# Last pass of a two-layer decode step with gradients: transposes of X one item later, V transposes, dq and gradients ahead of the products

## The chip, the cores and the metric

The kernel runs on one core of a Trainium2 chip. The metric is the device time of one execution in microseconds (us). The core has five engines that matter here: TensorE (PE in the profile; its weight loads are shown as PEld), VectorE (DVE), ScalarE (ACT), GpSimd (POOL) and SyncE (SP). Each works through its own list of instructions in the order in which it was built. Transfers between device memory and the core's on-chip memory (SBUF) are issued by SP, ACT and POOL and carried out by 16 DMA engines. TensorE writes to PSUM only; VectorE and ScalarE copy from there to SBUF (an "evacuation").

## What is computed

The reference runs two kinds of layer in turn, twice each (attention, feed-forward, attention, feed-forward), on one token, and then takes the gradient of the whole with respect to the inputs, the two caches and the weights.

```
x = x + A(layernorm(x))      # A: 32 query heads, 4 groups of 8 heads, caches K and V of 4 x 65536 x 128, weights wq, wo
x = x + B(layernorm(x))      # B: squared ReLU between w1 and w2
x = x + A(layernorm(x))
x = x + B(layernorm(x))
returns x and, for the incoming gradient grad_out, the gradients of x, K, V, wq, wo, w1, b1, w2, b2
```

Both attention layers use the same K and V, so the gradient of a cache is a sum of both layers' parts. K and V hold 67 MB each in bf16, and their gradients as much again: moving these is most of what the kernel does.

## The kernel before, in words

The kernel goes over the caches in passes: forward through layer 1 and layer 3, then backward through layer 3 (`attn_bwd3`), then a last pass, `attn_bwd4` (line 1050), which finishes layer 1 and writes the gradients of K and V for both layers. The change is in that last pass, which begins near 1198 us of the profiled execution and lasts to its end.

The last pass handles 4 groups of heads, and in each group 512 chunks of 128 cache rows, 8 chunks to an **item**: 64 items to a group and 256 in all. Four items make a **block** of 32 chunks (`UB4`, line 67), 64 blocks in all. A block's data comes as one load of 1 MB of V and one of 1 MB of K, issued on SP's queue (line 284) into areas that are used in turn (five, for most of the pass). What happens to an item:

- `vT` (line 1095): 8 transposes of V on TensorE into a PSUM tile `ps_tr` (line 1100), then one evacuation to one of three buffers (`small<-ps_tr`, lines 155 and 158).
- `vS` (line 1105): 8 matmuls of the transposed V with the output gradients of both layers, the **products**, into the one PSUM tile `ps_sc` (line 1123); a block's first product is preceded by one matmul that sets the tile to minus a correction (line 1114). After a block's last product, X, a 128 x 1024 tile in one of two buffers, is made of it: VectorE multiplies the products with the stored exponentials (lines 1132 and 1133) into one half, and GpSimd copies the exponentials themselves (lines 1134 and 1135) into the other half.
- `xT` (line 1141): once to a block, 8 transposes of X into a `ps_tr` tile (line 1146) and an evacuation. `ps_tr` has two buffers, shared with `vT`.
- `dq` (line 1151): 8 matmuls of K with X, summed over the group in PSUM (line 1163).
- `grads` (line 1178): 4 matmuls of transposed X with a small matrix (line 1191), two each into the two `ps_gg` tiles, each evacuated to a staging area (as f32 to bf16: `pair<-ps_gg` and `eT<-ps_gg`). After a block's last item the staged gradients of K and V leave as two stores of 1 MB on POOL's queue (lines 1211 and 1212).

The order of the program is that of `pipeline` (line 659): at each step i it calls each stage with item i less the stage's lag, in the order in which the stages are listed. Before, the list (line 1228) is `vT` with lag 0, `vS` with lag 2, and `k8` (which is `dq` and then `grads`) with lag 7; `xT` is called at the end of `vS` for a block's last item. The first items are called by hand (`opening`, line 1222), with the flag `opening` keeping `xT` out of `vS`. Between the steps come background tasks: rows of weights are fetched on ACT's or POOL's queue and multiplied on VectorE (line 433) and summed on ScalarE (line 434), and the weight gradients are made by small matmuls (lines 1244 and 1271) into the same two `ps_gg` tiles and stored from staging areas on POOL's queue (line 1275). Such a task is tied in behind what stands before it on its engine (`in_order`, line 640).

The program's order is not yet that of the engines. A planner takes it as a priority and, with estimated durations, writes each engine's list, so an instruction whose data it reckons late is passed by others. Which of VectorE and ScalarE makes an evacuation is decided in `evac` (line 145) as the program is written out, by two running sums of estimated load.

Of the kernel before, what the change touches and what calls it, by code (L numbers as in the profile page):

```python
# [18 lines left out]
def kernel(  # L19
# [47 lines left out]
    UB4 = 512 // R2  # L67
    IPG = C // 8
    TLEAD = 2
# [19 lines left out]
    def ps_tr():  # L89
        return PS["pool"].tile([P, 8, P], BF, name="ps_tr", tag="tr", bufs=2 if PS["pass4"] else 3)  # L90

    def ps_sc(shape):
        return PS["pool"].tile(shape, F32, name="ps_sc", tag="sc", bufs=1 if PS["pass4"] else 2)
# [51 lines left out]
    def evac(out, in_, kind="bf"):  # L145
        n = 1
        for d in in_.shape[1:]:
            n *= d
        if kind == "bf":
            ca, cd = 0.19 + n * 0.00081, 0.15 + n * 0.00053  # L150
        else:
            ca, cd = 0.19 + n * 0.00081, 0.15 + n * 0.00105
        if load["act"] + ca <= load["dve"] + cd:
            load["act"] += ca
            nc.scalar.copy(out=out, in_=in_)  # L155
        else:
            load["dve"] += cd
            nc.vector.tensor_copy(out=out, in_=in_)  # L158

    def add_load(act=0.0, dve=0.0):  # L160
        load["act"] += act
        load["dve"] += dve
# [477 lines left out]
    def in_order(fn, each=False):  # L640

        insts = nc.cur_bb.bb.instructions
        n0 = len(insts)
        before = {}
        fn()
        new = list(insts[n0:])
        want = {i.engine for i in new}
        k = n0 - 1
        while want - set(before) and k >= max(0, n0 - 4000):
            before.setdefault(insts[k].engine, insts[k])  # L650
            k -= 1
        for i in new:
            p = before.pop(i.engine, None)
            if p is not None:
                tc.add_manual_dep(i, p.name, NOSYNC, reason="in_order")
            if each:
                before[i.engine] = i

    def pipeline(n, stages, bg=None, done=()):
        maxlag = max(l for _, l in stages)  # L660
        for i in range(n + maxlag):
            for k, (fn, lag) in enumerate(stages):
                if (done[k] if done else 0) <= i - lag < n:
                    fn(i - lag)
            for fn in (bg or {}).pop(i, ()):
                in_order(fn)
        assert not bg, sorted(bg)

    def items_of(order, turn=0):

        return [(g, (c8 + (turn if g == order[0] else 0)) % C) for g in order for c8 in range(0, C, 8)]
# [378 lines left out]
    def attn_bwd4(La, Lb, oga, ogb, order, eTa, eTb, dqT, bg, group_done, streams, more_stage, tail, KT, vts):  # L1050
        lname = "B1"
        kit = items_of(order)
        n = len(kit)
# [7 lines left out]
        state = {("vt", idx): vt for idx, vt in enumerate(vts)}  # L1061
        kstream, vstream = streams

        def g_scores(g):
            sl = slice(g * R, (g + 1) * R)
            ndt4 = state[("ndt", g)] = NDT.next()
            nc.vector.tensor_copy(out=DOB[:, g, 0, 0:R], in_=oga.dOT[:, sl])
            nc.vector.tensor_copy(out=DOB[:, g, 0, R:R2], in_=ogb.dOT[:, sl])
            nc.vector.tensor_copy(out=ndt4[:, :, 0:R], in_=oga.nd2[:, sl].unsqueeze(1).to_broadcast([64, UB4, R]))
            nc.vector.tensor_copy(out=ndt4[:, :, R:R2], in_=ogb.nd2[:, sl].unsqueeze(1).to_broadcast([64, UB4, R]))  # L1070
# [34 lines left out]
        def vS(idx):  # L1105
            g, c8 = kit[idx]
            vt = state.pop(("vt", idx))
            for i in range(8):
                c = c8 + i
                slot = c % UB4  # L1110
                first = idx < UB4 // 8

                def minus(**flags):
                    nc.tensor.matmul(state["ps_dp"][:, :, :].rearrange("p c r -> p (c r)"), lhsT=sel2[:, :],
                                     rhs=state[("ndt", g)][:, :, :].rearrange("o c r -> o (c r)"), **flags)
                if slot == 0:
                    state["ps_dp"] = ps_sc([P, UB4, R2])
                    if not first:
                        minus(start=True, stop=False)
                ps_dp = state["ps_dp"]  # L1120
                last = slot == UB4 - 1
                w = min(4, UB4 - slot)
                nc.tensor.matmul(ps_dp[:, slot:slot + w, :].rearrange("p a b -> p (a b)"), lhsT=vt[:, i, :],  # L1123
                                 rhs=DOB[:, g, 0:w, :].rearrange("p a b -> p (a b)"), start=first and slot == 0, stop=last and not first, skip_group_check=first)
                if last:
                    if first:
                        minus(start=False, stop=True, skip_group_check=True)
                    c0 = c - slot
                    X = XS.next().rearrange("p (s r) -> p s r", r=R4)
                    ea = eTa[g][:, :, c0:c0 + UB4].rearrange("p h c -> p c h")  # L1130
                    eb = eTb[g][:, :, c0:c0 + UB4].rearrange("p h c -> p c h")
                    nc.vector.tensor_tensor(out=X[:, :, 0:R], in0=ps_dp[:, :, 0:R], in1=ea, op=ALU.mult)
                    nc.vector.tensor_tensor(out=X[:, :, R:R2], in0=ps_dp[:, :, R:R2], in1=eb, op=ALU.mult)
                    nc.gpsimd.tensor_copy(out=X[:, :, R2:3 * R], in_=ea)
                    nc.gpsimd.tensor_copy(out=X[:, :, 3 * R:R4], in_=eb)
                    add_load(dve=2 * (0.07 + UB4 * R * 0.0021))
                    state[("X", g, c0 // UB4)] = X
                    if not state.get("opening"):
                        xT(g, c0 // UB4)

        def xT(g, u):
            X = state[("X", g, u)]
            nblk = UB4 // 4
            pt2 = ps_tr()
            for bi in range(nblk):
                nc.tensor.transpose(pt2[:, bi, :], X[:, 4 * bi:4 * bi + 4, :].rearrange("p a b -> p (a b)"), ident_b[:, :])  # L1146
            xt = XT.next()
            evac(xt[:, 0:nblk, :], pt2[:, 0:nblk, :])
            state[(g, u)] = (X, xt)
# [67 lines left out]
        for i, a in zip((36, 2 * IPG + 14, n - 18), [pair[10]] + more_stage):  # L1217
            at(bg, i, lambda a=a: ST.areas.append(a))
        g0 = order[0]
        state["opening"] = True  # L1220
        g_scores(g0)
        opening = [(g_grads, g0), (vS, 0), (vT, 3), (vS, 1), (vT, 4), (vS, 2), (vT, 5), (vS, 3), (vT, 6), (xT, g0, 0), (grads, 0), (vS, 4),
                   (grads, 1), (vT, 7), (vS, 5), (grads, 2), (dq, 0), (dq, 1), (grads, 3), (dq, 2), (dq, 3)]
        assert len(vts) == 3 and UB4 == 4 * 8
        for fn, *args in opening:
            in_order(lambda: fn(*args), True)
        state["opening"] = False
        pipeline(n, [(vT, 0), (vS, TLEAD), (k8, TLEAD + UB4 // 8 + 1)], bg, (8, 6, 4))


    def rows_into(rows, cols, nj, twice=False):
# [190 lines left out]
    bg = {}  # L1422
# [170 lines left out]
    bg = {}  # L1593
# [31 lines left out]
    def the_end():  # L1625
        PS["end"] = True
        with tc.high_priority():
# [5 lines left out]
    last_tasks = gwq_tasks(ORD4[-1:], False)  # L1633
    after = [2, 0, 0, 1, 1, 1, 1, 1]
    attn_bwd4(L1, L3, og1, og3, ORD4, eT1, eT3, dqT1, bg, group_done, streams, more_stage,
              lambda i: [t for _, t in zip(range(after[i]), last_tasks)], KT4, vts)
    PS["last"] = True
# [34 lines left out]
```

## Time and profile before

| | us |
|---|---|
| median of 3 runs | 1976.6 (1975.8 to 1980.17) |
| the profiled execution's own time | 1977.79 |
| its span in the trace | 1976.0 |
| TensorE busy in the span | 1588.3 (80%) |
| VectorE busy | 1106.1 (56%) |
| ScalarE busy | 1032.0 (52%) |
| GpSimd busy | 206.2 (10%) |
| moved by DMA | 802.40 MB, mean 406 GB/s |

The span is what the trace covers; 1.8 us of the execution's own time lie around it. Busy times overlap, since the engines work side by side. A view by stage gives, for a stretch of the span, each engine's busy time with its number of instructions, the TensorE clock that was granted (1.00 is full speed), the mean busy share of the 16 DMA engines and the rate at which they moved data. A view of waits lists which engine's instructions of a line stood idle until which other instruction ended. A timeline lists the instructions of a stretch, runs of one kind merged, with the idle time before each and what ended it.

### The profile page before, as it was taken

What the parts mean: (1) busy time and instruction counts of PE and PEld (TensorE: products, weight loads), DVE (VectorE), ACT (ScalarE), POOL (GpSimd) and SP (SyncE); (2) the same over time, 40 slices, a digit from 0 to 9 for tenths busy, and PEclk for the clock granted to TensorE, in tenths of its full rate; (3) what the DMA queues carried; (4) which work ended last, traced back from release to release, by engine and by line L of the source; (5) the groups of instructions that cost most, each with busy time, mean ns of one, the idle gap of its engine ahead of it and who ended that gap; (6) DMA issues with size and microseconds to landing.
All of it is one profiled execution on the core that took longest, in us unless ns stands there. A gap on an engine that the chain in (4) does not pass through costs nothing. (4 is left out here: it accounts for less than half of the span.)

```text
span 1976.0 us, 65950 instructions
## 1 busy us (share of the span) xinstructions
PE 1588.3 (80%) x29997; PEld 1307.1 (66%) x30052; DVE 1106.1 (56%) x1823; ACT 1032.0 (52%) x1306; POOL 206.2 (10%) x370
## 2 busy tenths in 40 slices
PE   7887886579887857887878887888888878888886
PEld 6887775578787756777878775555555545445553
DVE  4544431146444313736454445787776678777876
ACT  3543332034433323435454446776776666677775
POOL 0000000000000000000000001223222222122222
PEclk9999998669999986999989987999999989898987
DMA  9999999989999999999999997999999999999998
GB/s 394 425 423 420 414 410 408 408 334 425 425 420 419 424 406 400 423 418 416 417 417 392 412 404 319 373 417 424 423 422 416 414 373 402 421 380 398 422 424 360
DMA packets 115651, 802.40 MB, mean 406 GB/s; under 512 B 11420, under 2 KB 11434, under 8 KB 57002
## 3 DMA queue, kind: packets, MB, share of 16 engines
q1 hardware_dynamic: 77530, 612.54, 75.2%
q0 software_dynamic: 29776, 170.94, 21.1%
q10 hardware_dynamic: 8064, 14.68, 2.0%
q8 instruction: 235, 3.85, 0.8%
q14 instruction: 46, 0.38, 0.0%
HBM read 628.18 MB, written 169.95 MB: 404 GB/s over the span
## 5 line engine op out<-in xcount | busy, mean ns | idle before, releaser
L158 DVE COPY small<-ps_tr 128x1024 bf16<-128x1024 bf16 x620 | 420.9, 688 | 306.0 <-PE ps_tr L747 178.4
L155 ACT COPY small<-ps_tr 128x1024 bf16<-128x1024 bf16 x385 | 386.7, 1014 | 373.2 <-PE ps_tr L747 210.1
L155 ACT CAST pair<-ps_gg 128x1024 bf16<-128x1024 f32 (+3 forms) x279 | 267.7, 972 | 124.7 <-PE ps_gg L1191 78.4
L158 DVE CAST pair<-ps_gg 128x1024 bf16<-128x1024 f32 (+2 forms) x213 | 252.7, 1189 | 108.0 <-PE ps_gg L1191 84.2
L747 PE MATMUL ps_tr<-ident_b,pair 128*128 128x128 bf16 x3328 | 245.7, 222 | 40.7 <-DMA pair<-in_A_k_cache_dram 32.1
L1191 PE MATMUL ps_gg<-pair,small 64*128 64x512 bf16 x1024 | 203.5, 407 | 54.6 <-ACT pair L155 14.5
L747 PEld LDWEIGHTS <-pair 128*128 128x128 bf16 x3328 | 196.0, 99 | 46.6 <-DMA pair<-in_A_k_cache_dram 36.0
L809 PE MATMUL ps_acc<-eT,pair 128*128 128x64 bf16 x3840 | 169.0, 204 | 45.8 <-DMA pair<-in_A_v_cache_dram 42.7
L1100 PE MATMUL ps_tr<-ident_b,pair 128*128 128x128 bf16 x2024 | 185.4, 229 | 16.4 <-DMA pair<-in_A_v_cache_dram 11.0
L766 PE MATMUL ps_sc<-L_qpad,small 128*128 128x64 bf16 (+7 forms) x3456 | 171.2, 192 | 19.9 <-ACT small L155 11.5
L809 PEld LDWEIGHTS <-pair 128*128 128x128 bf16 x3840 | 152.4, 103 | 50.0 <-DMA pair<-in_A_v_cache_dram 45.8
L1100 PEld LDWEIGHTS <-pair 128*128 128x128 bf16 x2024 | 130.5, 102 | 75.7 <-issue 57.7
L766 PEld LDWEIGHTS <-small 128*128 128x128 bf16 x3456 | 137.7, 98 | 31.9 <-ACT small L155 17.9
L434 ACT ACTIVATE pair<-pair 128x1024 bf16<-128x1024 bf16 (+1 forms) x105 | 118.5, 1130 | 43.7 <-DVE pair L433 42.7
L1191 PEld LDWEIGHTS <-small 64*128 64x128 bf16 x1024 | 58.7, 94 | 113.0 <-issue 84.4
L999 PE MATMUL ps_tr<-ident_b,pair 128*128 128x128 bf16 x1536 | 122.7, 229 | 12.8 <-DMA pair<-in_A_v_cache_dram 5.9
L999 PEld LDWEIGHTS <-pair 128*128 128x128 bf16 x1536 | 97.3, 103 | 30.5 <-issue 21.0
L1020 PE MATMUL ps_sc<-B_dOpad,small 128*128 128x64 bf16 (+7 forms) x2048 | 104.1, 194 | 15.6 <-DVE small L158 6.5
L1123 PE MATMUL ps_sc<-DOB,small 128*128 128x64 bf16 (+3 forms) x2048 | 113.1, 196 | 1.8 <-ACT small L1543 1.2
L155 ACT CAST eT<-ps_gg 128x1024 bf16<-128x1024 f32 (+1 forms) x92 | 90.9, 991 | 41.1 <-PE ps_gg L1191 13.8
L1123 PEld LDWEIGHTS <-small 128*128 128x128 bf16 x2048 | 89.1, 101 | 32.8 <-issue 27.4
L1163 PE MATMUL ps_acc<-small,pair 128*128 128x64 bf16 (+1 forms) x2048 | 107.3, 195 | 0.4
(293 smaller groups left out, 2060.3 us busy)
## 6 DMA issues: line engine op xcount, KB each, us to landing
pair<-in_A_v_cache_dram SPq DMA_DIRECT2D x74, 2048.0 KB, 20.0
pair<-in_A_k_cache_dram SPq DMA_DIRECT2D x63, 2048.0 KB, 20.4
out_dram<-pair POOLq DMA_DIRECT2D x104, 1024.0 KB, 18.0
pair<-in_A_v_cache_dram SPq DMA_DIRECT2D x80, 1024.0 KB, 11.6
pair<-in_A_k_cache_dram SPq DMA_DIRECT2D x78, 1024.0 KB, 10.5
eT<-in_A_k_cache_dram SPq DMA_DIRECT2D x21, 2048.0 KB, 20.7
eT<-in_A_v_cache_dram SPq DMA_DIRECT2D x12, 2048.0 KB, 27.1
out_dram<-eT POOLq DMA_DIRECT2D x41, 512.0 KB, 17.1
```

Source lines behind the costliest of these rows:

```text
L155: nc.scalar.copy(out=out, in_=in_)
L158: nc.vector.tensor_copy(out=out, in_=in_)
L434: nc.scalar.activation(out=view, in_=view, func=ACTF.Copy, accum_out=ycol)
L747: nc.tensor.transpose(pt[:, i, :], kb8[:, i, :], ident_b[:, :])
L766: nc.tensor.matmul(ps_s[:, slot:slot + w, :].rearrange("p a b -> p (a b)"), lhsT=kt[:, i, :], rhs=L["qpad"][:, g, 0:w, :].rearrange("p a b ...
L809: nc.tensor.matmul(ps_o[:, :, :].rearrange("p a b -> p (a b)"), lhsT=vb8[:, i, :], rhs=eT[g][:, :, c:c + 8], start=(c == 0), stop=(c == C ...
L999: nc.tensor.transpose(pt[:, i, :], vb8[:, i, :], ident_b[:, :])
L1020: nc.tensor.matmul(ps_dp[:, slot:slot + w, :].rearrange("p a b -> p (a b)"), lhsT=vt[:, i, :], rhs=dOpad[:, g, 0:w, :].rearrange("p a b -> ...
L1100: nc.tensor.transpose(pt[:, i, :], vb8[:, i, :], ident_b[:, :])
L1123: nc.tensor.matmul(ps_dp[:, slot:slot + w, :].rearrange("p a b -> p (a b)"), lhsT=vt[:, i, :], rhs=DOB[:, g, 0:w, :].rearrange("p a b -> p ...
L1163: nc.tensor.matmul(ps_dq[:, 0:w, :].rearrange("p a b -> p (a b)"), lhsT=kb8[:, i, :], rhs=X[:, sl:sl + w, :].rearrange("p a b -> p (a b)") ...
L1191: nc.tensor.matmul(pg[:, t2 * 512:(t2 + 1) * 512], lhsT=xt[64 * t2:64 * t2 + 64, blk0 + half, :], rhs=GG[64 * t2:64 * t2 + 64, :, :, :].re ...
```

## The change

`xT` is taken out of `vS` and becomes a stage of its own, `xT_behind`, with lag 3: a block's X is transposed one step after the products that made it. The stages of a step are listed in another order: V transposes, then dq and gradients, then the transposes of X, then the products. The numbers of the last argument are the first items that the pipeline (and not the hand-written opening) handles for each stage. Nothing is added to or taken from what is computed, loaded or stored.

```
                     state[("X", g, c0 // UB4)] = X
-                    if not state.get("opening"):
-                        xT(g, c0 // UB4)
+
+        def xT_behind(idx):
+            g, c8 = kit[idx]
+            if (c8 + 8) % UB4 == 0:
+                xT(g, c8 // UB4)
...
         g0 = order[0]
-        state["opening"] = True
         g_scores(g0)
...
         for fn, *args in opening:
             in_order(lambda: fn(*args), True)
-        state["opening"] = False
-        pipeline(n, [(vT, 0), (vS, TLEAD), (k8, TLEAD + UB4 // 8 + 1)], bg, (8, 6, 4))
+        pipeline(n, [(vT, 0), (k8, TLEAD + UB4 // 8 + 1), (xT_behind, TLEAD + 1), (vS, TLEAD)], bg, (8, 4, 4, 6))
```

`TLEAD` is 2 and `UB4 // 8` is 4.

## Prediction, made before the changed kernel had run

> **What bounds the kernel now.** I read four views in this order: the page's slices, the last pass by stage, its waits, and a timeline of one block.
>
> By stage (stretch, its length, then busy time and instructions of PE, PEld, DVE, ACT, POOL, granted clock, DMA share, GB/s):
>
> ```profile
> 1198.00:1240.00 42.00, 32.24 (x450) 22.74 (x449) 25.47 (x45) 25.55 (x27) 9.49 (x17) 0.80 0.76 298
> 1240.00:1300.00 60.00, 49.47 (x744) 34.01 (x743) 44.40 (x56) 45.27 (x52) 13.61 (x24) 0.94 0.96 379
> 1300.00:1520.00 220.00, 182.42 (x2513) 120.56 (x2524) 167.66 (x259) 155.63 (x177) 56.87 (x95) 0.95 1.01 423
> 1520.00:1600.00 80.00, 64.25 (x753) 40.46 (x765) 54.49 (x70) 56.80 (x66) 21.62 (x38) 0.92 1.01 413
> 1600.00:1640.00 40.00, 29.73 (x393) 20.00 (x394) 30.68 (x52) 24.07 (x30) 7.84 (x14) 0.88 0.93 363
> 1640.00:1740.00 100.00, 83.22 (x1037) 53.73 (x1044) 76.55 (x116) 71.59 (x93) 21.37 (x38) 0.89 1.01 408
> 1740.00:1800.00 60.00, 48.98 (x488) 28.42 (x494) 43.16 (x54) 44.66 (x50) 14.51 (x27) 0.86 0.97 380
> 1800.00:1940.00 140.00, 120.76 (x1639) 80.93 (x1649) 112.86 (x152) 109.06 (x125) 35.83 (x62) 0.96 1.02 420
> 1940.00:1976.00 36.00, 22.98 (x251) 11.59 (x248) 21.50 (x51) 17.61 (x30) 7.49 (x14) 0.68 0.84 337
> ```
>
> Read the DMA share first. In four stages (220 + 80 + 100 + 140 = 540 of 778 us) it is 1.01 or 1.02: the DMA engines have no idle time, while TensorE is busy for 80 to 86%. There the bound is the transfers, whose bytes the change leaves alone. DMA time is idle only in the others: 42 x 0.24 = 10.1 us, 60 x 0.04 = 2.4, 40 x 0.07 = 2.8, 60 x 0.03 = 1.8 and 36 x 0.16 = 5.8.
>
> TensorE's waits over the pass (who waited for whom: us in total, times, longest):
>
> ```profile
> PE ps_tr L1146 <- DVE small L1133: 20.9, 40, 1.2
> ...
> PE ps_tr L1146 <- POOL small L1134: 3.1, 4, 0.8
> PE ps_tr L1146 <- POOL small L1135: 2.7, 2, 1.4
> ```
>
> The wait that the change aims at is the transposes of X (line 1146) waiting for X: 20.9 + 3.1 + 2.7 = 26.7 us in 46 waits, a mean of 0.58.
>
> One block's turn on TensorE (start, length, the idle time before it in brackets):
>
> ```profile
> 1245.16 0.37 PE L1123 MATMUL ps_sc<-DOB,small 128*128 128x64 bf16 x8
> 1245.39 0.39 PE L1163 MATMUL ps_acc<-small,pair 128*128 128x64 bf16 x8
> 1245.71 0.79 PE L1191 MATMUL ps_gg<-pair,small 64*128 64x512 bf16 x4
> 1246.43 0.32 PE L1163 MATMUL ps_acc<-small,pair 128*128 128x64 bf16 x5
> 1247.21 0.61 PE L1146 MATMUL ps_tr<-ident_b,small 128*128 128x128 bf16 x8 [0.46 <-DVE small L1133]
> 1247.66 0.61 PE L1100 MATMUL ps_tr<-ident_b,pair 128*128 128x128 bf16 x8
> 1248.20 0.39 PE L1114 MATMUL ps_sc<-small,sel 64*128 64x512 bf16 x1
> ```
>
> The planner had already pushed the transposes of X behind dq, gradients and most of the next dq, and they still wait 0.46 us. From start to start, 8 products take 0.23 us (0.029 each), 8 V transposes 0.54 (0.068 each), 4 gradient matmuls 0.54 to 0.72 (0.135 each taken), a dq matmul about 0.03.
>
> **The change, part by part.**
>
> *Transposes of X later.* I counted, over all 64 blocks, what TensorE's built list has between a block's last product and its X transposes. Before, on average: 14.2 dq matmuls, 4.8 gradient matmuls, 1.8 V transposes, 1.1 products, 1.1 weight-gradient matmuls (line 1271). After: 9.0, 4.7, 9.8, 2.3, 1.5. The difference is +8.0 x 0.068 - 5.2 x 0.03 - 0.1 x 0.135 + 1.2 x 0.029 + 0.4 x 0.27 = 0.54 - 0.16 - 0.01 + 0.03 + 0.11 = 0.5 us more cover (0.27 for a line-1271 matmul is half the spacing of its pairs in the timeline). So each of the 46 waits shrinks by at most 0.5 us. With some shorter than that I take 0.4, or 0.4 / 0.58 = 0.69 of the idle time: 18 us of TensorE idleness go.
>
> What is that worth? Only what falls where DMA is idle. The same waits by stage: 1.2 us in 1212 to 1240, 3.7 in 1240 to 1300, 2.7 in 1600 to 1640, 0 in 1740 to 1800, 0.5 after 1940; 8.1 in sum, of which 0.69 is 5.6 us. In the first, the stores that wait behind it then hold the staging areas (VectorE waits 5.8 and ScalarE 6.2 us for `out_dram` before 1300), so a head start is partly stood out later: of 0.8 + 2.6 I take 1.2. At 1600 to 1640 a catch-up follows a 4.8 us stop: of 1.9 I take 1.0. At the end 0.3. **Sum: 2.5 us.** Ends: 0, if DMA takes all back, and 18, if the 1.01 of the four stages hides slack.
>
> What is next behind the moved transposes: the xt that they make is wanted by `grads` one step later, with a correction matmul (0.32), products (0.23), V transposes (0.54) and dq (0.23) in between, 1.3 us against an evacuation of 0.69 (VectorE) or 1.01 (ScalarE). It was more before; I cost it at 0, and at 64 x 0.2 = 13 us if ScalarE runs a copy behind, again nearly all under DMA.
>
> *Products last in the step.* Cyclically V transposes, products, dq, gradients become V transposes, dq, gradients, products: between two items' gradients stand the same three things, 1.0 us. What moves is the background: its matmuls (lines 1244, 1271), in the same two `ps_gg` tiles, came right behind the gradients and now come 0.23 us later, and the next gradients 0.23 us sooner behind them. Line 1271 waits 27 times for an evacuation, so up to 27 x 0.23 = 6 us either way. I take 0. V's own route gets longer by dq and gradients before its product is due: only slack.
>
> *Evacuations that change engine.* In the built lists 13 f32 evacuations go from VectorE to ScalarE and 13 bf16 ones come back. By the page's rows that is 13 x (1.19 - 0.69) = 6.5 us less VectorE work and about 13 x (0.97 - 1.01), -0.5 us, for ScalarE. Neither is full (113 and 109 of 140 us in the busiest stage); 0, at best part of the 6.5.
>
> *Queues.* SP's list has the same loads; in the second half several K and V loads swap with their neighbour, and each such load is at most one load's time off, 1 MB at 424 GB/s = 2.5 us, with a median landing of 11 us to hide it. On POOL's list the X copies of a dozen blocks trade places with a weight-gradient store that waits for its evacuation; some ahead, some behind. Line 1134 waits mostly for X's buffer, so it has steps in hand. 0, ends -2.5 and +2.5.
>
> The Trainium skill ("TensorE: Matmul & The Clock Gate", Part 1, on the clock gate) says that an idle window of about 3.4 us halves the clock and as long a busy one restores it. Here the granted clock is 1.00 in every 4 us slice from 1220 to 1256 in spite of X waits of 0.28 to 0.48, and 0.57 in the slice after a 3.42 us wait at 1252. By that rule the short waits that go (1.4 at most) return no clock; if the clock followed the busy share, 18 us less idleness would also raise it a little, which the rows do not bear out.
>
> **Sum**: 1977.79 (own time of the profiled execution, which is 1.2 above the median of 1976.6) - 2.5 = 1975.3; against the median **1974.1**, so I say 1974.
>
> **The rivals.** A change of 0.2%, 4.0 us, is about what a measurement can tell from none.
>
> *Compute binds more than the DMA share says* (chance 0.28). For: TensorE's waits on loads are 11.0 us in the pass, so the transfers rarely stop it directly, and the rate in 1640 to 1740 is 408, not 423. Against: slots are refilled as soon as they are free. It gives half of the 18 us, 9: about 1967.6.
>
> *Nothing arrives* (0.12): the planner's list had most of the cover already (1.7 us before the X transposes), and what goes turns up as waits for `ps_gg`. 1976 to 1979.
>
> *Rows come late, slower* (0.20). One row of wo or wq stops VectorE ahead of an evacuation that TensorE wants:
>
> ```profile
> 1593.13 9.22 DMA pair<-in_A_wo_dram
> ```
>
> VectorE stood 3.98 us for that row, gradients 4.85, and DMA shares of 0.87, 0.79, 0.87, 0.75 and 0.94 in the five 4 us slices after it lost 3.1 us. The row is fetched 4 items ahead. At the mean of 778 / 256 = 3.0 us an item that is 12 us; at TensorE's full pace in 1232 to 1240 (an item in about 1.8 us) it is 7. Faster items cross the 9.2 us sooner, at 2.3 us an item, and line 1611's task has the same lead. Two more such stops and none gone: +6.2, less 1: about 1982.
>
> **How the numbers follow.** The forecast, -1 to -4 us, has 0.40. Faster by over 0.2%: 0.28 and 0.06 of the forecast's edge, 0.34. Slower: 0.20 and 0.02 of the nothing case, 0.22. The rest, 0.44, is within 0.2%. Range: from 1965, past the first rival's middle, to 1983, past the last one's.
>
> **What would show it.** Right: line 1146's waits fall from 26.7 to under 12 us, the four full stages keep a DMA share of 1.01 and together last 540 us within 5, and the gain is before 1300 and around 1600. Wrong: if those stages shorten, DMA was not the bound; if line 1191's waits for its `ps_gg` evacuations (45.3 us in the same view) grow by what line 1146 loses, the second rival; if line 433 waits for rows in more places, the third.

## The result and the profile after

| | before | after |
|---|---|---|
| median, us | 1976.43 (1975.8 to 1980.17, 4 runs) | 1997.32 (1993.89 to 1999.04, 4 runs) |
| ratio to before, 95% interval | | 1.0101 [1.0085, 1.0116] |
| profiled execution's own time; span | 1977.79; 1976.0 | 1996.27; 1994.1 |
| mean granted TensorE clock | 0.914 | 0.905 |

The change costs 20.9 us; 1974 was forecast, with a range to 1983. Up to line 1137 the line numbers are unchanged; behind it the transposes of X have moved from line 1146 to 1149, dq from 1163 to 1166, the gradients from 1191 to 1194, and the weight gradients from 1244 and 1271 to 1245 and 1272.

**By stage**, the kernel after (columns as in the prediction):

```profile
1198.00:1240.00 42.00, 33.37 (x515) 23.67 (x513) 27.88 (x52) 28.83 (x31) 11.52 (x21) 0.96 0.85 324
1240.00:1300.00 60.00, 45.08 (x647) 30.35 (x644) 40.41 (x50) 39.93 (x46) 11.35 (x20) 0.89 0.90 338
1300.00:1520.00 220.00, 186.49 (x2555) 123.76 (x2553) 165.64 (x260) 153.73 (x177) 56.05 (x95) 0.94 1.01 422
1520.00:1600.00 80.00, 63.39 (x772) 40.42 (x770) 50.95 (x67) 55.49 (x63) 19.82 (x36) 0.92 1.01 406
1600.00:1640.00 40.00, 26.86 (x278) 16.58 (x278) 25.48 (x30) 20.38 (x26) 6.61 (x12) 0.81 0.91 342
1640.00:1740.00 100.00, 81.22 (x996) 51.87 (x995) 72.56 (x117) 64.51 (x83) 21.71 (x39) 0.89 0.93 359
...
1800.00:1940.00 140.00, 120.13 (x1470) 75.78 (x1469) 104.77 (x140) 106.00 (x120) 33.01 (x58) 0.90 1.00 409
```

Up to 1600 the two long stages have the DMA share that they had, 1.01. The stretch from 1640 to 1740 has lost it: 0.93 at 359 GB/s, where before had 1.01 at 408; and TensorE did only 278 matmuls from 1600 to 1640 where before it did 393. The same place is found by the start of the X transposes, block by block: for blocks 0 to 36 the kernel after is between 4.1 us earlier and 5.8 later than before, block 37 is 8.5 us later, block 40 15.9, block 43 25.9, and from block 49 on it stays some 20 us later (the last, 63, is 19.6 later). **The whole loss falls between about 1610 and 1725 us**, eight of 64 blocks.

TensorE's waits for X over the pass, the kernel after:

```profile
PE ps_tr L1149 <- DVE small L1133: 21.9, 24, 5.1
...
PE ps_tr L1149 <- POOL small L1135: 3.6, 5, 0.7
PE ps_tr L1149 <- POOL small L1134: 2.3, 4, 0.8
```

The waits went from 46 to 33, but their sum from 26.7 to 27.8 us, since two new ones are near 5 us long (5.11 and 4.86, in the timeline at 1601.77 and 1636.95). Without these two, 17.8 us are left. The cover that the change was to give arrived in part; the two long ones are something else.

VectorE's waits from 1600 to 1730, the kernel after, and behind it the kernel before:

```profile
DVE pair L433 <- DMA pair<-in_A_wo_dram: 13.7, 3, 4.7
...
DVE pair L433 <- DMA pair<-in_A_wq_dram: 4.9, 2, 4.0
```

```profile
DVE pair L433 <- DMA pair<-in_A_wo_dram: 4.0, 1, 4.0
```

Here is a stretch with three long stops of VectorE for rows of wo and one for a row of wq, where before had one in all. The stop at 1600 is like the one that before has at the same place (3.98 us, in the prediction); the others (4.53 us to 1619.53, 4.47 to 1635.62, and 3.99 to 1665.03 for the wq row) have none like them in before. What the first does, in VectorE's timeline of the kernel after:

```profile
1593.41 0.68 DVE L158 COPY small<-ps_tr 128x1024 bf16<-128x1024 bf16 x1
1594.01 1.22 DVE L158 CAST pair<-ps_gg 128x1024 bf16<-128x1024 f32 x1
1595.14 0.59 DVE L1132 TENSOR_TENSOR small<-ps_sc,eT 128x256 bf16<-128x256 f32 x1
1600.43 0.69 DVE L433 TENSOR_TENSOR pair<-pair 128x1024 bf16<-128x1024 bf16 x1 [4.70 <-DMA pair<-in_A_wo_dram]
1601.04 0.58 DVE L1133 TENSOR_TENSOR small<-ps_sc,eT 128x256 bf16<-128x256 f32 x1
1601.54 1.22 DVE L158 CAST pair<-ps_gg 128x1024 bf16<-128x1024 f32 x1
1602.67 0.68 DVE L433 TENSOR_TENSOR pair<-pair 128x1024 bf16<-128x1024 bf16 x1
```

The row product (line 433) stands between the two halves of X (lines 1132 and 1133). VectorE waits 4.70 us for that row, the second half of X comes 5 us late, and the transposes of X stop TensorE for 5.11 us. The second half needs the same products as the first, which had run; it waited only for its turn. The Trainium skill ("TensorE: Matmul & The Clock Gate", Part 1, on the architecture) says the queues of VectorE and ScalarE are strictly first in, first out; the rows agree, since line 1133 starts 5.3 us behind the end of line 1132's and only behind the row product.

And there are two row products, at 1600.43 and 1602.67. In the built list of the kernel after, **the first of them is the later row**: row 3 of the task stands ahead of row 2. Of the eight rows of this last wo task the list has 1 before 0, 3 before 2, 5 before 4 and 7 before 6, and two pairs of wq rows are swapped too; the list of the kernel before has no such pair. ScalarE's sums (line 434) and the fetches (line 891) stay in the order of the rows in both. Row 3 was fetched at 1590.88, row 2 at 1585.63, so VectorE waits for the younger transfer while the older row, fetched 5 us sooner, may be there (the trace has no landing of either).

Why the planner did so can be read from what each row is tied to. A background task is tied behind the last instruction on its engine in the program's order, that is, behind the last one of the step. Positions in VectorE's list, in the order of the rows:

```
row                                    0     1     2     3     4     5     6     7
before  position                     1377  1384  1389  1395  1396  1407  1413  1421
        tied behind (f: V transposes)  1376  1383  1388  1394  1387f 1406  1412  1420
after   position                     1380  1377  1393  1390  1405  1403  1418  1414
        tied behind (x: X transposes)  1379  1375x 1392  1385x 1404  1398x 1417  1409x
```

In the kernel before, seven of the eight ties are to a copy of the gradients (`pair<-ps_gg`), and those come one after the other. Rows come every second step, and X is made every fourth. With the transposes of X one item later **and** listed behind the gradients, their copy (`small<-ps_tr`) becomes the last VectorE instruction of every second one of the rows' steps. It stands ahead of the gradients' copy of the step of the row before, to which the even row is tied, and so the odd row is free to go ahead. The stop of 3.99 us at 1665.03 is another case: that wq row is behind its predecessor as it should be, but what it is tied behind is the second half of X, now last in its step, and it stands in the list straight behind the row before it (positions 1460 and 1461; in before 1457 and 1469).

### The profile page after: what moved, and what is told of

It is laid out like the page before. It is cut to its first block, busy times and chain, and to the rows that moved or that the text cites. A ratio compares the mean times of both kernels' runs of the same rounds, so it can differ in the third digit from the quotient of the medians.

```text
span 1994.1 us, 66009 instructions
## 1 busy us (share of the span) xinstructions
PE 1603.8 (80%) x30052; PEld 1317.9 (66%) x30052; DVE 1100.6 (55%) x1823; ACT 1027.2 (52%) x1306; POOL 204.6 (10%) x370
## 3 DMA queue, kind: packets, MB, share of 16 engines
q0 software_dynamic: 29776, 170.94, 20.9%
## 5 line engine op out<-in xcount | busy, mean ns | idle before, releaser
L158 DVE COPY small<-ps_tr 128x1024 bf16<-128x1024 bf16 x634 | 429.9, 687 | 317.3 <-PE ps_tr L747 176.6
L155 ACT COPY small<-ps_tr 128x1024 bf16<-128x1024 bf16 x371 | 373.2, 1014 | 363.3 <-PE ps_tr L747 209.6
L155 ACT CAST pair<-ps_gg 128x1024 bf16<-128x1024 f32 (+2 forms) x286 | 272.0, 965 | 124.0 <-PE ps_gg L1194 67.2
L158 DVE CAST pair<-ps_gg 128x1024 bf16<-128x1024 f32 (+1 forms) x206 | 247.4, 1202 | 103.0 <-PE ps_gg L1194 84.9
L1100 PE MATMUL ps_tr<-ident_b,pair 128*128 128x128 bf16 x2024 | 185.1, 230 | 17.7 <-DMA pair<-in_A_v_cache_dram 12.6
L434 ACT ACTIVATE pair<-pair 128x1024 bf16<-128x1024 bf16 (+1 forms) x105 | 118.6, 1132 | 55.7 <-DVE pair L433 55.4
L999 PE MATMUL ps_tr<-ident_b,pair 128*128 128x128 bf16 x1536 | 119.8, 226 | 11.3 <-DMA pair<-in_A_v_cache_dram 5.0
L155 ACT CAST eT<-ps_gg 128x1024 bf16<-128x1024 f32 (+1 forms) x98 | 96.5, 990 | 59.6 <-PE ps_gg L1272 34.7
L1123 PE MATMUL ps_sc<-DOB,small 128*128 128x64 bf16 (+3 forms) x2048 | 118.8, 197 | 0.3 <-ACT small L1544 0.3
L1166 PE MATMUL ps_acc<-small,pair 128*128 128x64 bf16 (+1 forms) x2048 | 117.2, 196 | 0.0
L1020 PE MATMUL ps_sc<-B_dOpad,small 128*128 128x64 bf16 (+7 forms) x2048 | 102.4, 193 | 15.1 <-DVE small L158 7.7
## 6 DMA issues: line engine op xcount, KB each, us to landing
pair<-in_A_k_cache_dram SPq DMA_DIRECT2D x63, 2048.0 KB, 19.6
```

The source lines that it names most:

```text
L434: nc.scalar.activation(out=view, in_=view, func=ACTF.Copy, accum_out=ycol)
L999: nc.tensor.transpose(pt[:, i, :], vb8[:, i, :], ident_b[:, :])
L1100: nc.tensor.transpose(pt[:, i, :], vb8[:, i, :], ident_b[:, :])
L1166: nc.tensor.matmul(ps_dq[:, 0:w, :].rearrange("p a b -> p (a b)"), lhsT=kb8[:, i, :], rhs=X[:, sl:sl + w, :].rearrange("p a b -> p (a b)") ...
```

## The experiments

Theory A: the tie moved, the rows are swapped or pushed together, come late for their product, and that is the loss. Theory B: the new order of the stages itself costs TensorE and VectorE the time, and the late rows are a sign of it. The table gives the ratio to the kernel before with its interval.

| run | edit | median, us | ratio |
|---|---|---|---|
| e1 | after, rows in order | 1981.63 | 1.0025 [1.001, 1.004] |
| e2 | before, wo rows swapped | 1988.33 | 1.0059 [1.004, 1.0078] |
| e3 | X transposes later alone | 1977.67 | 1.0002 [0.9993, 1.0012] |
| e4 | order of stages alone | 1984.2 | 1.0044 [1.003, 1.0058] |
| e5 | after, background tasks behind the gradients | 1977.21 | 1.0007 [0.9996, 1.0017] |
| e6 | after, wo rows fetched 6 items ahead | 1991.19 | 1.0072 [1.0055, 1.0088] |
| e7 | e4, background tasks behind the gradients | 1982.17 | 1.0025 [1.0014, 1.0035] |
| e8 | e3, rows in order | 1975.95 | 0.9996 [0.9984, 1.0007] |
| e9 | after, only the wo rows behind the gradients | 1980.55 | 1.0028 [1.0018, 1.0038] |
| e10 | after, five row fetches left out | 1978.74 | 1.0011 [1.0002, 1.0021] |
| e11 | before, the same fetches left out | 1971.05 | 0.9976 [0.9965, 0.9987] |

### e1: the rows kept in order

```
+    def in_row(p=None):
+        p, PS["row"] = PS.get("row"), nc.cur_bb.bb.instructions[-1] if PS["pass4"] else None
+        if p is not None: tc.add_manual_dep(PS["row"], p.name, NOSYNC, reason="rows")
...
-        nc.vector.tensor_tensor(out=view, in0=view, in1=vbc, op=ALU.mult)
+        nc.vector.tensor_tensor(out=view, in0=view, in1=vbc, op=ALU.mult); in_row()
```

> The changed kernel, with one thing more: in the last pass each row product (line 433) is tied behind the row product of the row before it, so that VectorE's list can no longer hold row k+1 ahead of row k. Nothing else is asked for. Theory A (rows swapped in pairs on VectorE, so that VectorE stops for a row that has not landed, some 20 us in all): no waits of line 433 for a row between 1600 and 1730 us beyond one or two, and a time of 1974 to 1982 us. Theory B (the new order of the stages itself costs TensorE and VectorE the time, the late rows being only a sign of it): 1990 us or more, with the blocks 36 to 43 still falling some 20 us behind the kernel before.

1981.63: 15.7 of the 20.9 us are gone with nothing but the order of the rows, and block 43 is 11.3 us late and not 25.9. Theory A's number came, at its upper edge. The tie keeps the rows in order but not apart: rows 0 and 1 stand next to each other in the list, and 4 and 5, and over the pass VectorE still waits 2.9 us for wo rows and 11.6 for wq rows (half of it, 5.8, in one stop, at the wq row named above).

### e2: the kernel before with the wo rows swapped

```
+    PS = {}; PAIRS = (17, 19, 21, 23)
...
+        if p is not None and (e == "a" or PS["k"] in PAIRS): tc.add_manual_dep(*((PS[e], p.name) if e == "a" else (p, PS[e].name)), NOSYNC, reason="rows")
...
+        nc.vector.tensor_tensor(out=view, in0=view, in1=vbc, op=ALU.mult); in_row("v")
+        nc.scalar.activation(out=view, in_=view, func=ACTF.Copy, accum_out=ycol); in_row("a")
```

(`p` is the product of the row before, `PS["v"]` the row's own; for the four pairs the tie goes the other way round. The tie with `e == "a"` keeps ScalarE's sums in order.)

> The kernel before, with its old order of stages, but the eight row products of the last wo task swapped in pairs on VectorE (row 1 ahead of row 0, 3 ahead of 2 and so on); ScalarE's sums stay in the old order. Theory A: VectorE stops at most of the four swapped rows for 3 to 5 us each, the time rises by 8 to 18 us, to 1984 to 1994 us. Theory B: the swap alone costs less than 4 us, 1974 to 1980 us.

1988.33, 11.7 us more by the ratio (0.0059 x 1976.5), with the old order of stages: theory A's number, and theory B said under 4. But not by the way that I had expected: VectorE has no stop at a wo row here at all. The planner put each pair in the place of its second row, so both rows have landed. ScalarE's timeline shows what it cost instead, the fetches of that task:

```profile
1590.80 0.33 ACTq L891 DMA_DIRECT2D pair<-in_A_wo_dram  x1
1591.97 0.33 ACTq L891 DMA_DIRECT2D pair<-in_A_wo_dram  x1
1608.08 0.33 ACTq L891 DMA_DIRECT2D pair<-in_A_wo_dram  x1
1609.36 0.33 ACTq L891 DMA_DIRECT2D pair<-in_A_wo_dram  x1
1625.12 0.36 ACTq L891 DMA_DIRECT2D pair<-in_A_wo_dram  x1
1626.23 0.34 ACTq L891 DMA_DIRECT2D pair<-in_A_wo_dram  x1
```

There are three row buffers, and a buffer is free for the next row only when the product and then the sum of its row are done. A pair that is multiplied together frees its buffers together, so from row 2 on the fetches go out in twos, 17 us apart, where before has one every 5 to 11 us, and the task ends late: its last product is at 1642.3 and not 1629.4. Behind it, from 1640 to 1680, the DMA share is 0.82 where before had 1.00, and from block 41 on the blocks are some 13 us later than before. So a swap can cost without any stop. That the late fetches are the cause is read from these times; no run takes them away alone.

### e3 and e4: each part alone

```
e3: pipeline(n, [(vT, 0), (xT_behind, TLEAD + 1), (vS, TLEAD), (k8, TLEAD + UB4 // 8 + 1)], bg, (8, 4, 6, 4))
e4: pipeline(n, [(vT, 0), (k8, TLEAD + UB4 // 8 + 1), (vS, TLEAD)], bg, (8, 4, 6))     # xT at the end of vS, as before
```

> One part of the change alone: the transposes of X one item later, with the stages otherwise in the order V transposes, X transposes, gradients and dq, products. The planner's list for VectorE holds one swapped pair of rows in place of six. Theory A: 1973 to 1982 us (at most one stop of some 5 us). Theory B, if the later transposes carry the loss: 1990 us or more; if the order of the stages carries it: as the kernel before, within 3 us.

> The other part alone: the products put behind the gradients (V transposes, dq, gradients, products), with the transposes of X where the kernel before has them, straight behind X. The planner's list for VectorE holds one swapped pair of rows. Theory A: 1973 to 1982 us. Theory B, if the order of the stages carries the loss: 1990 us or more; if the later transposes carry it: as the kernel before, within 3 us.

The expectation of e3 names its order wrongly: it is V transposes, X transposes, products, dq, gradients. Its 1977.67 is no difference from before (1.0002 [0.9993, 1.0012]). e4's 1984.2 is 2 us above the range that I gave to theory A and 6 below theory B's. By the ratios the parts alone cost 0.4 + 8.7 = 9.1 us together, and the change 20.0. More than half comes only of the two together, which theory B, a price for each place of a stage, doesn't explain, and the table of ties does: only with both does the X transposes' copy fall last in every second of the rows' steps. e3 has one swapped pair among the wo rows and e4 none there; each of the two has one pair in place of six.

### e5 and e7: the tie put back, the stages left

```
-    def pipeline(n, stages, bg=None, done=()):
-        maxlag = max(l for _, l in stages)
+    def pipeline(n, stages, bg=None, done=(), tasks_behind=None):
+        maxlag, tasks_behind = max(l for _, l in stages), len(stages) - 1 if tasks_behind is None else tasks_behind
...
-            for fn in (bg or {}).pop(i, ()):
-                in_order(fn)
+                for task in (bg or {}).pop(i, ()) if k == tasks_behind else ():
+                    in_order(task)
...
+        pipeline(n, [(vT, 0), (k8, TLEAD + UB4 // 8 + 1), (xT_behind, TLEAD + 1), (vS, TLEAD)], bg, (8, 4, 4, 6), 1)
```

> The changed kernel with the background tasks of a step issued straight behind the stage of dq and gradients, and not at the end of the step. In the changed kernel every second row product of the last wo task is tied behind the evacuation of the X transposes, which the planner runs earlier than the gradients' evacuations that the row before it is tied to; here every row is tied behind a gradients' evacuation again, as in the kernel before, and VectorE's list holds no row ahead of its predecessor and no two close together. Theory A1 (the tie is the whole cause, spacing included): 1972 to 1979 us, no wait of line 433 over 3 us between 1600 and 1730. Theory A2 (the swapped order is most of it, but something of the stage order is left, as the 5 us of the run with rows in order would have it): 1980 to 1984. Theory B (the stage order itself): 1990 or more.

> The order of the stages alone (V transposes, dq, gradients, products with the transposes of X straight behind X), with the background tasks issued behind the gradients; VectorE's list holds no swapped pair of rows, where the run of the order alone has one, at which VectorE stopped for 7.4 us. Theory A1: the 7.7 us of that run go, 1974 to 1979 us. Theory A2 or B, if the order costs something by itself: 1981 us or more.

e5 is the deciding run: every stage as in the kernel after, only the background issued one place earlier in the step. 1977.21, ratio 1.0007 [0.9996, 1.0017]: **all but at most 3.4 us of the 20.9 are gone**, and A1 holds. The rows are apart again in VectorE's timeline of e5:

```profile
1590.78 0.68 DVE L433 TENSOR_TENSOR pair<-pair,pair 128x1024 bf16<-128x1024 bf16 x1
...
1597.92 0.68 DVE L433 TENSOR_TENSOR pair<-pair 128x1024 bf16<-128x1024 bf16 x1
...
1604.62 0.81 DVE L433 TENSOR_TENSOR pair<-pair 128x1024 bf16<-128x1024 bf16 x1
```

No idle time stands behind any of them, and VectorE waits for rows 0.9 us in the whole pass. What the transfers make of it, in the stretch from 1600 to 1720: before, after, e5.

```profile
1600.00:1720.00 120.00, 96.73 (x1245) 63.68 (x1256) 92.26 (x140) 82.98 (x105) 26.94 (x48) 0.90 0.98 394
```

```profile
1600.00:1720.00 120.00, 90.68 (x1029) 56.97 (x1030) 80.07 (x119) 72.89 (x92) 22.75 (x41) 0.84 0.91 348
```

```profile
1600.00:1720.00 120.00, 99.59 (x1219) 64.49 (x1229) 91.72 (x143) 87.10 (x106) 28.01 (x50) 0.90 0.99 403
```

The kernel after moves (394 - 348) x 120 = 5.5 MB less there than before, 13 us at 424 GB/s, and e5 moves more than before. That fits stops that cost by draining the transfers: waiting engines free no areas to load into. It is read from the rate; no run holds the transfers up in another way. The deepest part, 0.70 at 275 GB/s from 1660 to 1680, lies not at the wo stops but around the wq stop at 1665.

e7 gives 1982.17, where A1 said at most 1979: with the order of stages alone, 4.9 us [2.8, 6.9] stay although no row is swapped. There the transposes of X come straight behind X with the products last, and TensorE waits 27.1 us in 43 waits for X (line 1133), against 20.9 in 40 before. e5 has 16.9 in 26. That would fit a price of the products last that the later transposes pay back. But the execution that was profiled took 1977.21 us, no more than the one of before (1977.79), so its waits cannot account for the median's 4.9 us. Where these come from stays open.

### e6: the rows fetched earlier

```
-    og1.later(vbx1, ORD4[3], bg, 2 * IPG + 8, 2, wo_rows, 4, nc.scalar)
+    og1.later(vbx1, ORD4[3], bg, 2 * IPG + 8, 2, wo_rows, 6, nc.scalar)
```

> The changed kernel with one number changed: the rows of the last wo task are fetched 6 items ahead of their product in place of 4, the most that three row buffers hold. The six swapped pairs stay in VectorE's list. Theory A in the form that the rows come late for their product: the stops of 4.7, 4.5 and 4.5 us at the wo rows fall to under 1.5 us each, and the time by 8 to 14 us, to 1983 to 1989 us. If instead the swap costs by holding both buffers of a pair until the second row is there, so that nothing is in flight: the stops go, but the fetches still come in pairs, and the time stays within 5 us of the changed kernel, 1992 to 2002.

Neither: 1991.19, about 6 us less than after, and the stops are still there, 13.9 us in 4 waits for wo rows. The reason is in the timelines of e6, ScalarE's first and VectorE's behind it:

```profile
1589.06 1.06 ACT L434 ACTIVATE pair<-pair 128x1024 bf16<-128x1024 bf16 x1
...
1590.24 0.33 ACTq L891 DMA_DIRECT2D pair<-in_A_wo_dram  x1
```

```profile
1600.60 0.69 DVE L433 TENSOR_TENSOR pair<-pair 128x1024 bf16<-128x1024 bf16 x1 [5.49 <-DMA pair<-in_A_wo_dram]
```

The fetch of row 3 was wanted two items sooner, but it goes out at 1590.24, right behind the sum of row 0, whose buffer it takes; in the kernel after it went out at 1590.88. Here a larger lead was worth nothing to that row, since the buffer is what its fetch waits for, and the swap makes the first row of a pair give its buffer back late. Where the 6 us come from I did not find; the profiled execution took 1995.43 us, as long as the one of the kernel after (1996.27), and can't show it.

### e8: the later transposes with the rows in order

The edits of e1 and e3 together.

> The later transposes of X alone (V transposes, X transposes, products, dq, gradients; the run before with this order was named with the products last by mistake), with each row product tied behind the one before it, so that its one swapped pair goes. If the shorter waits of the X transposes (11.9 us in that run against 20.9 before) are worth what was forecast for them: 1973 to 1975 us. If they are worth nothing, because the transfers bound the pass: 1976 to 1979.

1975.95, and the interval of the ratio, -3.2 to +1.4 us, holds both answers. TensorE's waits for X have come down to 11.7 us in 25 waits for line 1133, and 1.1 for line 1135: less than half of the 26.7 before, and a gain of at most 3 us for it. But much of the idle time has only moved. Before, and behind it e8:

```profile
PE ps_tr L1100 <- DMA pair<-in_A_v_cache_dram: 11.0, 7, 5.1
...
PE ps_sc L1114 <- DVE small L1133: 1.3, 6, 0.4
```

```profile
PE ps_tr L1100 <- DMA pair<-in_A_v_cache_dram: 13.5, 8, 5.8
PE ps_tr L1149 <- DVE small L1133: 11.7, 25, 1.4
...
PE ps_sc L1114 <- DVE small L1133: 4.6, 9, 1.4
```

The correction matmul (line 1114) now waits for the same second half of X, 3.3 us more. With every releaser counted, the V transposes (line 1100) wait 22.0 us in place of 15.1 and the gradients 53.1 in place of 48.8. All of TensorE's waits in the pass sum to 125 us before and 122 in e8: of the 13.9 us that X no longer costs, about 3 are gone.

### e9: only the wo rows put back

```
-                at(bg, i0 + k * step, lambda k=k: one(k))
+                at(bg, (i0 + k * step, 1) if step == 2 else i0 + k * step, lambda k=k: one(k))
```

(`pipeline` issues tasks with such a key behind its stage 1, the gradients.)

> The changed kernel with only the eight row products of the last wo task issued straight behind the gradients; all other background tasks stay at the end of the step, so the two swapped pairs among the wq rows stay and the four of wo go. If the cost goes with the wo pairs: 1977 to 1984 us, with the stops of 3.99 and 0.90 us at wq rows still there. If the wq pairs carry it: 1989 us or more.

1980.55: the four pairs of wo carry 16.8 us, 80% of the loss, and the other 3.3 us to e5 go with the tasks that stay, the two swapped pairs of wq rows and the wq row behind X among them. VectorE's waits from 1600 to 1730 in e9 have the wq stops alone:

```profile
DVE pair L433 <- DMA pair<-in_A_wq_dram: 7.2, 3, 3.8
```

### e10 and e11: the swap kept, the rows not fetched

```
                 box[k] = rows.next()
-                queue.dma_start(out=box[k], in_=A_wo[g * GD + k * P:g * GD + (k + 1) * P, :])
+                if step != 2 or k < 3: queue.dma_start(out=box[k], in_=A_wo[g * GD + k * P:g * GD + (k + 1) * P, :])
```

> The changed kernel, but of the eight rows of the last wo task only the first three are fetched; the other five products are made of what their buffers hold, so that part of the computation is left out. VectorE's list keeps all six swapped pairs. The bytes left out are 1.3 MB, 3.1 us at 424 GB/s. If the pairs cost by waiting for rows that have not landed: the two later wo stops (4.5 us each) go, the one at 1600 (row 3) too, and the time falls to 1976 to 1985 us. If the swapped places in the list cost by themselves, whatever the rows do: 1990 to 1997.

> The control to the run without fetches: the kernel before with the same five fetches left out. 3.1 us fewer of transfers and the stop of 4.0 us at a wo row gone, of which something under 4 us is worth time: 1970 to 1975 us.

With all six swapped pairs still in the list, but nothing to wait for at the last five rows of wo, the kernel after takes 1978.74, 18.6 us less. The same cut takes 5.1 us from the kernel before (e11, 1971.05 against 1976.11 for the runs of before beside it), of which 3.1 are the bytes by the estimate above. So 13.5 us of the loss come with the fetched rows, and the swapped places of these rows cost little by themselves. The 7.7 us that still lie between e10 and e11 have a place in the traces, the wq rows: VectorE waits for them in e10, and not at all from 1600 to 1730 in e11.

```profile
DVE pair L433 <- DMA pair<-in_A_wq_dram: 6.9, 2, 6.0
```

The stretch around it, in e10 and then in e11:

```profile
1640.00:1660.00 20.00, 12.98 (x178) 8.75 (x177) 9.54 (x17) 10.86 (x16) 2.25 (x4) 0.83 0.68 270
```

```profile
1640.00:1660.00 20.00, 16.78 (x221) 11.05 (x219) 16.20 (x23) 16.27 (x21) 5.26 (x10) 1.00 1.01 421
```

The stop of 6.0 us is at the wq row behind X, and e11 moves (421 - 270) x 20 = 3.0 MB more in these 20 us, 7 us at 424 GB/s. No run moves that row alone, so this part is argued.

## Why the prediction was wrong, point by point

**The symptom of the loss was named; its cause and its size were not.** The third rival, "Rows come late, slower", had the line (433), the engine, the consequence (VectorE stops ahead of what TensorE wants, DMA drains) and the sign to look for, "if line 433 waits for rows in more places". It had 0.20 and 1982. It was reasoned by pace, items that get faster and cross the 9.2 us of a row's landing sooner, and priced at two more stops, 6.2 us. Two more stops at wo rows did come, and a long one at a wq row, but for another reason: e5 has the same stages without the stops. That the rival's sign came true is luck.

**The step that failed** is "Products last in the step", in the sentence "What moves is the background: its matmuls (lines 1244, 1271)". The background's matmuls were followed; its row products were not. Each task is tied behind the last instruction of its engine in the step, so a change of which stage is last changes what the rows are tied to. The prediction counted TensorE's built list around the X transposes and looked through SP's and POOL's, but not VectorE's list for line 433, where the six swapped pairs stand. That step's "I take 0", with 6 us to either side, should have been 13 to 17 us for the wo rows (e10, e9) and some 3 for the rest (e9 to e5).

**X transposes later**: 0.5 us less of each wait, -2.5 us of time. Measured in the old order of the other stages (e8), the waits fall by 13.9 us of 26.7, less than the 18 forecast and to 12.8, short of the sign "under 12"; the time falls by 0.8 us [-3.2, +1.4]. The size, 2.5, cannot be told from 0. The rule used, that only idleness in stages without full DMA is worth time, was not put to the test: the idle time did not go, it moved to other waits (125 us in all before, 122 in e8). That is the second rival, "Nothing arrives", and in part by its own sign: the four evacuations of `ps_gg` keep the gradients waiting 49.6 us in e8, where before had 45.3. The first rival's gain of 9 us, "Compute binds more than the DMA share says", came in no run (at most 3.2 in e8), but with the idle time only moved it was not tested either. At the opening, where 1.2 us were to come from, nothing came: in the kernel after block 7 is 3.0 us late and block 15 4.4, in e5 block 15 is 3.5 late, both with one wait of over 6 us of the gradients for ScalarE's copy near 1250, where the stores hold the staging areas.

**Products last**, for the matmuls: e7 against before puts +4.9 us [2.8, 6.9] on the order without the later transposes; with them (e5) there is no difference that can be measured. Whether the 4.9 are the matmuls' no run shows. The medians lie inside the 6 us that were allowed.

**Evacuations that change engine**: in the kernel after VectorE's busy time is 1100.6 and ScalarE's 1027.2 us, 5.5 and 4.8 less than before (6.5 and 0.5 were forecast); neither engine was busy for more than 56% of the span, and no gain in time can be seen from it.

**Queues**: TensorE's waits for loads of V are 11.0 us before, 12.6 after, 16.6 in e5 and 13.5 in e8. Whether the loads that swap on SP's list make them longer no run shows; the time of e5 leaves at most 3.4 us for all that the new stages cost together, so a large term is ruled out and the 0 is not shown.

**The four full stages** were to keep a DMA share of 1.01 and last 540 us. In the same stretches of time three have 1.00 or 1.01; 1640 to 1740 fell to 0.93. How long each stage's own work lasted was not measured. A loss of transfers was made up only in part: block 43 is 25.9 us late and the last block 19.6. In e9, block 43 is 18.0 us late, with stops at wq rows alone, and the last block 3.0, so a delay there can also be made up; why the one of the wo rows stays is not shown.

**The clock.** Around the stop shown above, 4 us slices of the kernel after, granted clock third from the end:

```profile
1596.00:1600.00 4.00, 0.61 (x10) 0.29 (x6) 0.00 (x0) 2.04 (x3) 1.71 (x3) 1.00 1.03 426
1600.00:1604.00 4.00, 2.23 (x11) 1.14 (x11) 3.36 (x5) 0.62 (x1) 0.00 (x0) 0.61 1.00 424
1604.00:1608.00 4.00, 4.00 (x51) 2.86 (x51) 2.01 (x2) 0.78 (x3) 0.00 (x0) 0.54 0.79 256
1608.00:1612.00 4.00, 3.69 (x54) 2.48 (x50) 2.75 (x4) 3.47 (x5) 1.70 (x3) 1.00 0.93 319
```

TensorE waits from 1596.66 to 1601.77. For 4.2 us of it the clock stays at 1.00, and the transfers go on at 426 GB/s, from the loads already issued. In slices of 1 us the clock is 0.92 from 1600 and 0.50 from 1601, and full again by 1608. So most of the price comes behind the stop: from 1601.77 some 5.9 us at half the clock, 2.9 us of TensorE at full speed, and 256 and 319 GB/s, (168 + 105) x 4 us = 1.1 MB or 2.6 us of transfers. A stop of 4.7 us is therefore not paid off when the row lands. The kernel before pays the same at its one stop (0.72, 0.50 and 0.50 in the three slices from 1596), so it is the further stops that make a difference. The prediction used the Trainium skill's rule ("TensorE: Matmul & The Clock Gate", Part 1: an idle window of about 3.4 us halves the clock) to say that the short waits that go return no clock; the same rule, for a wait of 5 us, agrees with these rows.

## What to carry to other kernels

In this kernel, a task that is tied to "whatever comes last before it" is moved by every reordering of what comes before it: after such a change, compare for each engine the order of the instructions that wait for transfers with the order in which those are issued. A swapped pair cost here the stop, the clock behind it, and, with a ring of three buffers, later fetches of the rows that follow. When two halves of a change cost less apart (here 9.1 us) than together (20.0), look for what only the combination selects (here the last VectorE instruction of every second step).

## What the runs showed that I had not expected

Swapped rows cost 11.7 us without a single stop at a wo row (e2), where the fetches go out in twos. A lead of six items in place of four moved the fetch of the row that VectorE asks for first by 0.64 us (1590.24 against 1590.88), since its buffer set the time (e6). And a row of this task, 256 KB, takes a median of 8.6 us (before), 9.3 (e5) and 9.8 (e6) from issue to landing, counted over the rows whose landing the trace has (in the kernel after only two, 3.5 and 8.7 us), though its bytes alone would be 0.6 us at 424 GB/s. Here a lead has to cover the landing, and not the bytes alone.
